# Attention and a gated feed-forward layer on one Trainium2 core: the planner's rules for VectorE and GpSimd rewritten

## The chip, the cores and the metric

The program runs on one NeuronCore of a Trainium2 chip. The core has TensorE (PE, matrix products), VectorE (DVE), ScalarE (ACT) and GpSimd (POOL) for elementwise work, and SyncE (SP), whose queue issues every transfer here. They work on SBUF and on PSUM, where TensorE leaves its results; GpSimd works on SBUF only. The metric is the device time of one execution in microseconds (us). The time before is 734.29 us, the median of 3 runs (733.88 to 735.38).

## The reference

```python
def _attn_ref(q, k, v):                       # 4 batches, 8 heads, 768 tokens, 64 wide
    block, window = (32, 16)
    k_sum = k.reshape(B, H, nb, block, D).max(axis=3)
    v_sum = v.reshape(B, H, nb, block, D).mean(axis=3)
    scores_l = scale * np.matmul(q, k.transpose(0, 1, 3, 2))      # used where |i - j| < window
    scores_s = scale * np.einsum('bhsd,bhnd->bhsn', q, k_sum) + np.log(block)
    ...
    a = softmax over [masked scores_l, scores_s]
    return np.matmul(a, np.concatenate([v, v_sum], axis=2))

def _moe_ref(x, w_gate, w_val, w_out):        # 3072 tokens, 512 -> 1536 -> 512; weights are float64
    g = x @ w_gate
    silu = g * (1.0 / (1.0 + np.exp(-g)))
    return (silu * (x @ w_val) @ w_out).astype(np.float32)
```

Each token attends to its neighbours within 16 places and to the 24 pooled blocks of its sequence. The result is the input `x` of a gated feed-forward layer.

## The kernel before

The four batches of the attention are four stages of the layer. Attention goes in 32 units: `k` counts half sequences (two per batch, 384 tokens), `u` counts pairs of heads. A unit is: the scores (`SC`, tile `sc`), per query tile a maximum with bias on VectorE (`ttr`, L467), exponentials on ScalarE (L481), the reciprocal of the sum (L499), a scaling of `p` by it (`nrm`, L502), transposes (`PP`, tile `pp`) that are copied out to `pt`, and the product with the values (`XO`, tile `xo`). Small copies put pooled keys (`kw<-ks`) and pooled values (`vw<-vs`) beside the windows.

The layer's operands are split into a high and a low part (`xh`/`xl`, `hh`/`hl`, the two halves of `w` and `o`), and a product is three matmuls. The float64 weights come as pairs of words, and five steps of `decode` turn each block into float32: one on ScalarE (L747) and four on VectorE (L751, L757, L764, L770), for twelve blocks `m_w` of 1024 columns and twelve `m_o` of 512. Then `split` makes `w` or `o`.

Batch 0 multiplies plainly (`u_plain`: `g` and `v` of 12 matmuls each, then `a` = silu(`g`) times `v`). Meanwhile `w_first` forms four sums and differences of the quarters of each `m_w` and stores them (`sf`, and `wa`). Batches 1 to 3 use these in a scheme that needs seven products instead of eight (`u_seven`, L888): the products `p` leave PSUM through VectorE steps that read PSUM (`v`, `u`, two of the `c`) and ScalarE copies (`s`), and the steps `c22` (`c<-v,u`), `a<-c,a`, `hh` and `hl` follow in SBUF. Before each of these batches `x_operands` builds the operands from the attention's result `xf` by differences and splits (`t`, `xf<-xf,xf`, `xh`, `xl`). Every third block `j`, `downs` multiplies by the output weights (L948, tile `acc`, six row tiles), and each result is added from PSUM into `part` (L335), which frees its PSUM bank.

The order is not the one in which the code stands. Each piece becomes a step of a plan, with the engines that can do it and a cost for each, and `order` calls `run` three times. `run` is a list scheduler: it gives every step an engine and a start by estimated costs, waits for buffers included, and instructions are then issued in the order of the starts. TensorE keeps two fixed lines (the layer's steps, and the attention's at its side) and takes whichever can start first. The other engines take, of the steps that are ready, the one with the earliest due time. A step that several engines can do goes to the one that would end it first, with a handicap per engine:

```python
BIAS = {DVE: 1.2, ACT: 0.6}
...
mine = soon + s.engines[e] + BIAS.get(e, 0)
if any(max(free[x], at[s]) + c + BIAS.get(x, 0) < mine - 1e-9 for x, c in s.engines.items() if x != e):
    continue
```

`cost` gives a step of two SBUF inputs and 384 columns 0.57 us on VectorE and 1.03 us on GpSimd. These numbers decide only the order and the engine; on the chip an engine works off its own queue in that order, waiting for the data that each instruction needs. Early in the program `warm_up` puts filler matmuls where the plan lets TensorE idle.

Of the kernel before, what the change touches and what calls it, by code (L numbers as in the profile page):

```python
# [197 lines left out]
def run(steps, line, late):  # L198
# [30 lines left out]
    while n:  # L229
        best = None  # L230
        for e, waiting in ready.items():
# [47 lines left out]
def body(ctx, tc, qP, kP, vT, vP, wgv, wo, bias, ident, mean, out):  # L279
# [68 lines left out]
    def add_dma(name, nbytes, out, in_, reads, writes):  # L348
        plan.add(name, {DMA: nbytes / 0.36e6}, lambda e: nc.sync.dma_start(out(), in_()), reads, writes)
# [30 lines left out]
    def a_pool_keys(b, u):  # L380
# [57 lines left out]
    def a_scores(k, u):  # L438
# [71 lines left out]
    def a_transposes(k, u):  # L510
# [6 lines left out]
        for g in range(2):  # L517
# [689 lines left out]
```

## Time and profile before

| | before |
|---|---|
| median of 3 runs | 734.29 us |
| profiled execution | 735.51 us, of which the span from first to last instruction is 733.7 us |
| TensorE busy | 691.4 us, 94% |
| VectorE busy | 457.6 us, 62% |
| ScalarE busy | 368.8 us, 50% |
| GpSimd busy | 408.0 us, 56% |
| DMA | 150.17 MB, mean 205 GB/s |
| chain that ended last | PE 58%, DVE 19%, DMA 9%, POOL 5%, ACT 5% |

Busy time is the union of an engine's instructions. Durations of neighbouring instructions on one engine overlap a little, so a step costs its engine the distance from start to start. In a group's row stand its count, its busy time, the mean of one instruction in nanoseconds, and the idle time of the engine before it with what ended it. The time of the instructions depends on the stage, so the tables of stretches matter more than the means over the run.

### The profile page before, as it was taken

What the parts mean: (1) busy time and instruction counts of PE and PEld (TensorE: products, weight loads), DVE (VectorE), ACT (ScalarE), POOL (GpSimd) and SP (SyncE); (2) the same over time, 40 slices, a digit from 0 to 9 for tenths busy, and PEclk for the clock granted to TensorE, in tenths of its full rate; (3) what the DMA queues carried; (4) which work ended last, traced back from release to release, by engine and by line L of the source; (5) the groups of instructions that cost most, each with busy time, mean ns of one, the idle gap of its engine ahead of it and who ended that gap; (6) DMA issues with size and microseconds to landing.
All of it is one profiled execution on the core that took longest, in us unless ns stands there. A gap on an engine that the chain in (4) does not pass through costs nothing.

```text
span 733.7 us, 13256 instructions
## 1 busy us (share of the span) xinstructions
PE 691.4 (94%) x4902; PEld 618.3 (84%) x4902; DVE 457.6 (62%) x995; ACT 368.8 (50%) x861; POOL 408.0 (56%) x387
## 2 busy tenths in 40 slices
PE   8787988999889999999999989999999999999997
PEld 7576876889779897897979879898989889989896
DVE  3799999888983858465755956343544942234342
ACT  3567744775655446565755527574754513322121
POOL 3767737656695946256564937263554834344342
PEclk9999899999999999999999999999999999999999
DMA  8999833758874359587583738284643546254422
GB/s 293 314 311 311 270 131 127 258 202 304 279 236 161 113 207 329 182 288 249 195 282 122 268 137 293 77 254 133 225 154 115 187 166 221 102 201 143 158 101 87
DMA packets 73329, 150.17 MB, mean 205 GB/s; under 512 B 25968, under 2 KB 48176, under 8 KB 67120
## 3 DMA queue, kind: packets, MB, share of 16 engines
q1 hardware_dynamic: 73264, 149.32, 59.8%
q8 instruction: 39, 0.64, 0.4%
q14 instruction: 26, 0.21, 0.1%
HBM read 114.70 MB, written 34.60 MB: 203 GB/s over the span
## 4 chain that ended last, share of the span: by engine, by line
PE 58%; DVE 19%; DMA 9%; POOL 5%; ACT 5%; issue 3%; SPq 1%; POOLq 0%; DVEq 0%; ACTq 0%
PE p L888 30%; PE acc L948 19%; DMA s<-sf 3%; PE g L865 2%; DVE m_o L764 2%; PE v L865 2%; PE xo L554 2%; PE sc L450 2%; DMA kt<-in_kP 2%; DVE xl_T L335 2%; PE pp L523 2%; DMA raw_o<-in_wo 1%; DVE m_w L764 1%; POOL m_w L335 1%; DVE m_w L751 1%
## 5 line engine op out<-in xcount | busy, mean ns | idle before, releaser
L948 PE MATMUL acc<-o,hh 128*128 128x512 f32 x576 | 186.5, 405 | 7.8 <-DVE part L335 6.1
L948 PEld LDWEIGHTS acc<-o,hh 128*128 128x128 f32 x576 | 106.4, 192 | 32.4 <-DVE part L335 7.4
L948 PE MATMUL acc<-o,hl 128*128 128x512 f32 x288 | 115.5, 401 | 6.0 <-POOL hl L335 5.9
L888 PE MATMUL p<-xh_T,s 128*128 128x384 f32 x432 | 120.1, 340 | 0.2 <-POOL s L335 0.2
L335 POOL TENSOR_TENSOR hl<-a,hh 128x384 fp32r<-128x384 f32 x88 | 99.7, 1140 | 30.0 <-ACT hh L330 16.1
L481 ACT ACTIVATE p<-p,nm 128x120 f32<-128x120 f32 x192 | 73.6, 385 | 31.1 <-DVE nm L467 30.6
L888 PE MATMUL p<-xh_B,wa 128*128 128x384 f32 x288 | 86.7, 341 | 0.0
L335 POOL TENSOR_TENSOR c<-v,u 128x384 f32<-128x384 f32 x31 | 32.7, 1056 | 91.1 <-DVE u L335 89.4
L335 POOL TENSOR_TENSOR a<-c,a 128x384 f32<-128x384 f32 x56 | 58.0, 1040 | 41.5 <-ACT a L847 23.5
L888 PEld LDWEIGHTS p<-xh_T,s 128*128 128x128 f32 x432 | 78.9, 188 | 1.6 <-issue 0.6
L335 DVE TENSOR_TENSOR part<-acc,part 128x512 f32<-128x512 f32 x72 | 48.1, 685 | 44.6 <-PE acc L948 44.5
L502 POOL TENSOR_TENSOR p<-p,ri 128x720 f32<-128x720 f32 x30 | 44.8, 1492 | 53.4 <-DVE ri L499 53.2
L335 DVE TENSOR_TENSOR c<-p,u 128x384 f32<-128x384 f32 x72 | 39.8, 554 | 54.1 <-PE p L888 52.9
L948 PEld LDWEIGHTS acc<-o,hl 128*128 128x128 f32 x288 | 55.2, 192 | 20.9 <-POOL hl L335 8.8
L888 PE MATMUL p<-xl_T,s 128*128 128x384 f32 x216 | 72.3, 335 | 0.0
L865 PE MATMUL g<-xh_B,w 128*128 128x384 f32 x192 | 56.4, 354 | 5.0 <-DVE w L335 2.2
L330 ACT COPY s<-p 128x384 f32<-128x384 f32 x60 | 28.5, 477 | 59.6 <-PE p L888 59.2
L467 DVE CUSTOM_DVE_ANT_0 p<-sc,bias_sb 128x120 f32<-128x120 f32 x192 | 41.6, 276 | 25.7 <-PE sc L450 25.3
L335 DVE TENSOR_TENSOR v<-p,s 128x384 f32<-128x384 f32 x36 | 20.0, 556 | 60.0 <-PE p L888 55.8
L335 POOL TENSOR_TENSOR m_w<-m_w 128x256 f32<-128x256 f32 x48 | 48.4, 1007 | 14.3 <-DVE w L335 11.1
L865 PE MATMUL v<-xh_B,w 128*128 128x384 f32 x192 | 55.0, 347 | 0.0
L888 PEld LDWEIGHTS p<-xh_B,wa 128*128 128x128 f32 x288 | 53.1, 188 | 1.6 <-issue 0.9
(118 smaller groups left out, 1514.1 us busy)
## 6 DMA issues: line engine op xcount, KB each, us to landing
wa<-wa SPq DMA_DIRECT2D x36, 768.0 KB, 4.3
s<-ss SPq DMA_DIRECT2D x24, 1024.0 KB, 7.6
raw_w<-in_wgv SPq DMA_DIRECT2D x12, 1024.0 KB, 6.9
ss<-s SPq DMA_DIRECT2D x12, 1024.0 KB, 5.8
wa<-w SPq DMA_DIRECT2D x12, 768.0 KB, 4.5
kw<-in_kP SPq DMA_DIRECT2D x28, 288.0 KB, 5.8
vw<-in_vP SPq DMA_DIRECT2D x28, 288.0 KB, 5.2
kt<-in_kP SPq DMA_DIRECT2D x16, 400.0 KB, 5.4
```

The costliest lines, as they stand in the source:

```text
L330: nc.scalar.copy(out, in_)
L335: vector[e].tensor_tensor(out=out, in0=a, in1=b, op=op)
L450: nc.tensor.matmul(make(sc[h])[s * QT : (s + 1) * QT, c * KC : (c + 1) * KC], make(q)[hs, qs], make(kw)[hs, i, :], start=True, stop=True,)
L467: nc.vector.tensor_tensor_reduce(out=make(p)[:, i, :], in0=make(sc[g])[:, c * KC : (c + 1) * KC], in1=make(bias_sb)[:, 0 if n == 0 else 2 ...
L481: nc.scalar.activation(out=make(p)[:, i, :], in_=make(p)[:, i, :], func=AF.Exp, scale=-1.0, bias=make(nm)[:, i : i + 1], accum_out=make(sm ...
L502: vector[e].tensor_tensor(out=make(p), in0=make(p), in1=make(ri).rearrange("p (n o) -> p n o", o=1).broadcast_to([P, NT, KC]), op=ALU.mult,)
L523: nc.tensor.transpose(make(pp)[:KC, c * P : (c + 1) * P], make(p)[:, g * NT // 2 + c, :], make(id_sb))
L554: nc.tensor.matmul(ps[hs, qs], v, make(pt)[:, h, qs], start=True, stop=True)
L764: lambda e: nc.vector.scalar_tensor_tensor(out=bits(), in0=high(), scalar=-0x40000000, in1=bits(), op0=ALU.bitwise_and, op1=ALU.bitwise_or ...
L865: nc.tensor.matmul(t[:, :TOK], a, x, start=u == 0 and n == 0, stop=u == NP - 1 and n == 2)
L888: nc.tensor.matmul(t[:, :TOK], a, x, start=first and kk == 0 and n == 0, stop=kk == 1 and n == 2, skip_group_check=not first,)
L948: nc.tensor.matmul(ps, a, w, start=j == js[0] and m == 0, stop=j == js[-1] and m == 2)
```

## The change

The planner gets a rule for VectorE and GpSimd. A step has a flag `port`: true if it reads nothing from PSUM (with exceptions set by hand: the pooling reductions and the reciprocal). In the plan, a GpSimd step starts only when the last VectorE step with `port` has ended (less 0.2 us), and such a VectorE step only when the last GpSimd step has. The choice of the engine looks at the start that this rule allows, and a step that would have to wait 1 us is ranked 1 us later. The handicaps become 0 for VectorE and ScalarE and 0.3 for GpSimd. The four weight sums become four steps, each for GpSimd or VectorE. Some costs are set anew (a transfer, TensorE's steps), filler matmuls are put in for the plan's first 110 us instead of 60, and the step `v` of `u_seven` is renamed.

```diff
-    def add(self, name, engines, do, reads=(), writes=(), table=None):
+    def add(self, name, engines, do, reads=(), writes=(), table=None, port=None):
         step = Step(name, engines, do, len(self.steps))
+        if port is None:
+            port = not any((b[0] if isinstance(b, tuple) else b).ring.pool == "psum" for b in reads)
+        step.port = port
         step.table, step.side, step.gate, step.slack = table, self.side, self.gate if self.side else None, self.slack if self.side else 0.0
 ...
 EARLY = 6.0
-BIAS = {DVE: 1.2, ACT: 0.6}
+BIAS = {DVE: 0.0, ACT: 0.0, POOL: 0.3}
+WAIT = 1.0
+HOLD = 0.2
 ...
     free = {PE: 0.0, DVE: 0.0, ACT: 0.0, POOL: 0.0, DMA: 0.0}
+    held = {DVE: 0.0, POOL: 0.0}
     table, place = None, [0, 0]
 ...
             else:
+                def start_of(x, s):
+                    t = max(free[x], at[s])
+                    if x == POOL:
+                        t = max(t, held[DVE])
+                    elif x == DVE and s.port:
+                        t = max(t, held[POOL])
+                    return t
+
                 soon = max(free[e], min(at[s] for s in waiting))
 ...
                         continue
+                    go = start_of(e, s)
                     if len(s.engines) > 1:
-                        mine = soon + s.engines[e] + BIAS.get(e, 0)
-                        if any(max(free[x], at[s]) + c + BIAS.get(x, 0) < mine - 1e-9 for x, c in s.engines.items() if x != e):
+                        mine = go + s.engines[e] + BIAS.get(e, 0)
+                        if any(start_of(x, s) + c + BIAS.get(x, 0) < mine - 1e-9 for x, c in s.engines.items() if x != e):
                             continue
-                    k = late[s] + (2.0 if s.table and s.table != table else 0.0)
+                    k = late[s] + (2.0 if s.table and s.table != table else 0.0) + WAIT * (go - soon)
                     if pick is None or (k, s.n) < (pick[1], pick[2].n):
-                        pick = (soon, k, s)
+                        pick = (go, k, s)
                 if pick is None:
 ...
         (start, _, s), e = best
+        if e == POOL or e == DVE and s.port:
+            start = max(start, held[POOL if e == DVE else DVE])
         for x in s.engines:
 ...
         s.idle = start - free[e]
+        if e == POOL or e == DVE and s.port:
+            held[e] = s.end - HOLD
         free[e] = s.end - (0.06 if e in (DVE, ACT, POOL) else 0.0)
 ...
     def add_dma(name, nbytes, out, in_, reads, writes):
-        plan.add(name, {DMA: nbytes / 0.36e6}, lambda e: nc.sync.dma_start(out(), in_()), reads, writes)
+        plan.add(name, {DMA: nbytes / 0.33e6}, lambda e: nc.sync.dma_start(out(), in_()), reads, writes)
 ...
-        def sums(e):
-            tt(e, at("A22"), at("A21"), at("A22"), ALU.add)
-            minus(e, at("A21"), at("A11"), at("A21"))
-            minus(e, at("A11"), at("A22"), at("A11"))
-            minus(e, at("A12"), at("A12"), at("A11"))
-
-        plan.add(f"sums w{j}", {POOL: 2.9}, sums, (), (m,))
+        for to, x, y, op in (("A22", "A21", "A22", ALU.add), ("A21", "A11", "A21", ALU.subtract), ("A11", "A22", "A11", ALU.subtract), ("A12", "A12", "A11", ALU.subtract)):
+            plan.add(
+                f"sum{to} w{j}", on((POOL, DVE), "tt", HALF), lambda e, to=to, x=x, y=y, op=op: tt(e, at(to), at(x), at(y), op), (), (m,)
+            )
         sf = SF[j] = buf("dram", f"sf{j}", [P, NC], f"sf{j}")
 ...
     for s in order(plan.steps):
-        if s.engine == PE and s.start < 60.0:
+        if s.engine == PE and s.start < 110.0:
             spare[0] = min(10, max(0, int((s.idle - 0.5) / 0.25)))
```

The costs of TensorE's steps change in the same manner as that of the transfer: `SC` 1.0 to 0.95, `PP` 0.36 to 0.38, `XO` 1.1 to 1.0, a product's matmul 0.1755 to 0.1745, one of `D` 0.231 to 0.229. `pool`, `vpool` and `rcp` get `port=False`.

In the built program VectorE has 1297 rows of instructions instead of 996, GpSimd 103 instead of 356, ScalarE 493 instead of 532, SP 281 in both. Three places show it.

VectorE in batch 0, where the first half of its rows of `u_plain` for the second 384 tokens stand (`m_o5` is the sixth block of output weights under `decode`, `a_0_0_1` the product of silu and `v` of block 0, second half). Before:

```order
L757 TENSOR_SCALAR m_o5_1122<-m_o5_1122 128x512
L764 SCALAR_TENSOR_TENSOR m_o5_1122<-raw_o5_706,m_o5_1122 128x512
L335 TENSOR_TENSOR xl_B22_0_1_1148<-xo_1_3_1125,xh_B22_0_1_1142 128x384
L770 SCALAR_TENSOR_TENSOR m_o5_1122<-raw_o5_706,m_o5_1122 128x512
L751 TENSOR_SCALAR m_o6_1151<-m_o6_1151 128x512
L757 TENSOR_SCALAR m_o6_1151<-m_o6_1151 128x512
L764 SCALAR_TENSOR_TENSOR m_o6_1151<-raw_o6_728,m_o6_1151 128x512
L770 SCALAR_TENSOR_TENSOR m_o6_1151<-raw_o6_728,m_o6_1151 128x512
L751 TENSOR_SCALAR m_o7_1188<-m_o7_1188 128x512
L757 TENSOR_SCALAR m_o7_1188<-m_o7_1188 128x512
L335 TENSOR_TENSOR a_0_0_1_1185<-v_0_1_1172,a_0_0_1_1185 128x384
L764 SCALAR_TENSOR_TENSOR m_o7_1188<-raw_o7_734,m_o7_1188 128x512
```

and now:

```order
L770 TENSOR_SCALAR m_o5_1173<-m_o5_1173 128x512
L354 TENSOR_TENSOR a_0_0_1_1170<-v_0_1_1157,a_0_0_1_1170 128x384
L776 TENSOR_SCALAR m_o5_1173<-m_o5_1173 128x512
L770 TENSOR_SCALAR m_o6_1177<-m_o6_1177 128x512
L783 SCALAR_TENSOR_TENSOR m_o5_1173<-raw_o5_775,m_o5_1173 128x512
L354 TENSOR_TENSOR hl_0_0_1_1216<-a_0_0_1_1170,hh_0_0_1_1197 128x384
L789 SCALAR_TENSOR_TENSOR m_o5_1173<-raw_o5_775,m_o5_1173 128x512
L776 TENSOR_SCALAR m_o6_1177<-m_o6_1177 128x512
L783 SCALAR_TENSOR_TENSOR m_o6_1177<-raw_o6_782,m_o6_1177 128x512
L354 TENSOR_TENSOR a_0_1_1_1219<-v_1_1_1203,a_0_1_1_1219 128x384
L354 TENSOR_TENSOR o5_1222<-m_o5_1173,o5_1222 128x512
L789 SCALAR_TENSOR_TENSOR m_o6_1177<-raw_o6_782,m_o6_1177 128x512
```

Against the product `a_0_0_1` the decode steps stand two blocks of output weights later, and the splits `hl` and `o5`, which were on GpSimd, stand between them.

VectorE before batch 2 (`xf_2_...`, `t3_2_...` and `xl_..._2_...` are that batch's operands, `a_1_11_1` and `hl_1_11_1` the last block of batch 1, `acc_1_3_0` its last product with the output weights). Before:

```order
L335 TENSOR_TENSOR xf_2_2_0_3746<-xf_2_2_0_3746,xf_2_0_0_3316 128x384
L335 TENSOR_TENSOR a_1_11_1_4717<-c22_1_11_4659,a_1_11_1_4717 128x384
L335 TENSOR_TENSOR xl_T4_2_0_4737<-xf_2_2_0_3746,xh_T4_2_0_4726 128x384
L335 TENSOR_TENSOR xl_B22_2_1_4743<-xf_2_3_1_4721,xh_B22_2_1_4728 128x384
L335 TENSOR_TENSOR xf_2_1_1_4332<-xf_2_1_1_4332,xf_2_1_0_3524 128x384
L335 TENSOR_TENSOR xf_2_1_0_3524<-xf_2_3_1_4721,xf_2_1_1_4332 128x384
L335 TENSOR_TENSOR xf_2_3_0_3928<-xf_2_3_0_3928,xf_2_1_0_3524 128x384
L335 TENSOR_TENSOR xl_T2_2_1_4775<-xf_2_1_0_3524,xh_T2_2_1_4767 128x384
L335 TENSOR_TENSOR part_1_0_3308<-acc_1_3_0_4710,part_1_0_3308 128x512
L335 TENSOR_TENSOR part_1_1_3311<-acc_1_3_1_4730,part_1_1_3311 128x512
L335 TENSOR_TENSOR part_1_2_3327<-acc_1_3_2_4747,part_1_2_3327 128x512
```

and now:

```order
L354 TENSOR_TENSOR t3_2_1_4736<-xf_2_3_1_4718,xf_2_1_1_4338 128x384
L354 TENSOR_TENSOR xl_T2_2_0_4740<-xf_2_0_0_3311,xh_T2_2_0_4705 128x384
L354 TENSOR_TENSOR hl_1_11_1_4751<-a_1_11_1_4720,hh_1_11_1_4738 128x384
L354 TENSOR_TENSOR xl_T3_2_1_4753<-t3_2_1_4736,xh_T3_2_1_4742 128x384
L354 TENSOR_TENSOR xf_2_1_1_4338<-xf_2_1_1_4338,xf_2_1_0_3531 128x384
L354 TENSOR_TENSOR xl_B21_2_1_4759<-xf_2_3_0_3936,xh_B21_2_1_4680 128x384
L354 TENSOR_TENSOR xf_2_1_0_3531<-xf_2_3_1_4718,xf_2_1_1_4338 128x384
L354 TENSOR_TENSOR part_1_0_3304<-acc_1_3_0_4709,part_1_0_3304 128x512
L354 TENSOR_TENSOR part_1_1_3316<-acc_1_3_1_4729,part_1_1_3316 128x512
L354 TENSOR_TENSOR part_1_2_3328<-acc_1_3_2_4744,part_1_2_3328 128x512
L354 TENSOR_TENSOR xl_T2_2_1_4790<-xf_2_1_0_3531,xh_T2_2_1_4775 128x384
L354 TENSOR_TENSOR xf_2_2_0_3741<-xf_2_2_0_3741,xf_2_0_0_3311 128x384
```

The three `part` stand ahead of the last operand steps, behind which they stood, and steps that GpSimd did (`t3`, `hl_1_11_1`, `xl_T3_2_1`) are among VectorE's.

GpSimd from the start of batch 1 (`c22`, `a` and `hl` of its first blocks; `s` a block's stored sums; `p_4_0` a unit's weights of attention). Before:

```order
L335 TENSOR_TENSOR c22_1_0_2969<-v_1_0_2959,u2_1_0_2967 128x384
L335 TENSOR_TENSOR a_1_0_0_2977<-c21_1_0_2985,a_1_0_0_2977 128x384
L335 TENSOR_TENSOR a_1_0_1_3006<-c22_1_0_2969,a_1_0_1_3006 128x384
L335 TENSOR_TENSOR hl_1_0_0_3037<-a_1_0_0_2977,hh_1_0_0_3020 128x384
L332 COPY kw_4_2_3043<-ks_2_2_2150 128x6x24
L335 TENSOR_TENSOR hl_1_0_1_3059<-a_1_0_1_3006,hh_1_0_1_3052 128x384
L335 TENSOR_TENSOR s_1_2_3022<-s_1_2_3022 128x1024
L502 TENSOR_TENSOR p_4_0_3015<-p_4_0_3015,ri_4_0_3118 128x720
L335 TENSOR_TENSOR a_1_1_0_3097<-c21_1_1_3099,a_1_1_0_3097 128x384
L335 TENSOR_TENSOR a_1_1_1_3123<-c22_1_1_3089,a_1_1_1_3123 128x384
L335 TENSOR_TENSOR hl_1_1_0_3172<-a_1_1_0_3097,hh_1_1_0_3168 128x384
L335 TENSOR_TENSOR hl_1_1_1_3185<-a_1_1_1_3123,hh_1_1_1_3174 128x384
```

and now:

```order
L354 TENSOR_TENSOR a_1_0_0_2973<-c21_1_0_2985,a_1_0_0_2973 128x384
L354 TENSOR_TENSOR hl_1_0_0_3024<-a_1_0_0_2973,hh_1_0_0_3015 128x384
L354 TENSOR_TENSOR a_1_0_1_3017<-c22_1_0_2965,a_1_0_1_3017 128x384
L354 TENSOR_TENSOR a_1_1_0_3103<-c21_1_1_3121,a_1_1_0_3103 128x384
L354 TENSOR_TENSOR a_1_1_1_3141<-c22_1_1_3094,a_1_1_1_3141 128x384
L351 COPY kw_5_0_3375<-ks_2_0_2893 128x6x24
L521 TENSOR_TENSOR p_4_2_3356<-p_4_2_3356,ri_4_2_3440 128x720
L351 COPY kw_5_1_3573<-ks_2_1_2931 128x6x24
L354 TENSOR_TENSOR s_1_5_3520<-s_1_5_3520 128x1024
L354 TENSOR_TENSOR c22_1_4_3615<-v_1_4_3563,u2_1_4_3605 128x384
L351 COPY vw_4_2_3318<-vs_2_3197 24x768
L354 TENSOR_TENSOR a_1_5_1_3761<-c22_1_5_3751,a_1_5_1_3761 128x384
```

What stood in the first list and is missing in the second is in VectorE's queue.

More of the change, by code (lines that the diff above doesn't have):

```diff
@@ L387, in do @@
             )
-        plan.add(f"pool({b},{u})", {DVE: 0.95}, do, (kt,), (ks,))
+        plan.add(f"pool({b},{u})", {DVE: 0.95}, do, (kt,), (ks,), port=False)
     def a_queries(k, u):
@@ L453, in do @@
                     )
-        plan.add(f"SC({k},{u})", {PE: 1.0}, do, (q, kw), sc)
+        plan.add(f"SC({k},{u})", {PE: 0.95}, do, (q, kw), sc)
     def a_softmax(k, u):
@@ L498, in a_softmax @@
         )
-        plan.add(f"rcp({k},{u})", {DVE: 0.18}, lambda e: nc.vector.reciprocal(out=make(ri), in_=make(sm)), (sm,), (ri,))
+        plan.add(f"rcp({k},{u})", {DVE: 0.18}, lambda e: nc.vector.reciprocal(out=make(ri), in_=make(sm)), (sm,), (ri,), port=False)
         def scale(e):
@@ L523, in turn @@
                     nc.tensor.transpose(make(pp)[:KC, c * P : (c + 1) * P], make(p)[:, g * NT // 2 + c, :], make(id_sb))
-            plan.add(f"PP{g}({k},{u})", {PE: 0.36}, turn, (p, id_sb), (pp,))
+            plan.add(f"PP{g}({k},{u})", {PE: 0.38}, turn, (p, id_sb), (pp,))
             add_copy(
@@ L554, in do @@
                     nc.tensor.matmul(ps[hs, qs], v, make(pt)[:, h, qs], start=True, stop=True)
-        plan.add(f"XO({k},{u})", {PE: 1.1}, do, reads, (xo,))
+        plan.add(f"XO({k},{u})", {PE: 1.0}, do, reads, (xo,))
     def load_first_values(x):
@@ L628, in do @@
             )
-        plan.add(f"vpool({b},{u})", {DVE: 0.95}, do, (vt,), (vr,))
+        plan.add(f"vpool({b},{u})", {DVE: 0.95}, do, (vt,), (vr,), port=False)
     def a_turn_values(b, u):
@@ L891, in do @@
                     )
-        plan.add(f"{name}({b},{j})", {PE: 6 * 0.1755}, do, [src] + sum(ops, []), (acc,))
+        plan.add(f"{name}({b},{j})", {PE: 6 * 0.1745}, do, [src] + sum(ops, []), (acc,))
     def u_seven(b, j):
@@ L907, in u_seven @@
         v = tmp("v")
-        add_tt(f"v({b},{j})", (DVE,), TOK, full(v), of(p5), full(s7), ALU.add, (p5, s7), (v,))
+        add_tt(f"vv({b},{j})", (DVE,), TOK, full(v), of(p5), full(s7), ALU.add, (p5, s7), (v,))
         product(b, j, "P6", "S2", "T2", p6, True, True)
@@ L952, in piece @@
             reads = sum(([*HH[b, j, hf], O[j]] for j in todo), [])
-            plan.add(f"D{n}({b},{g},{t})", {PE: 0.231 * 3 * len(todo)}, do, reads, (acc,))
+            plan.add(f"D{n}({b},{g},{t})", {PE: 0.229 * 3 * len(todo)}, do, reads, (acc,))
         def finish():
```

## The prediction

> **What bounds the kernel now.** I read the busy times of the page, then the table of busy time by stretch, then who releases TensorE, then single instructions where it idles.
>
> ```profile
> PE 691.4 (94%) x4902; PEld 618.3 (84%) x4902; DVE 457.6 (62%) x995; ACT 368.8 (50%) x861; POOL 408.0 (56%) x387
> ...
> 0.00:40.00 40.00, 31.70 (x401) 26.78 (x402) 22.74 (x80) 18.02 (x63) 19.95 (x38) 0.96 0.90 302
> 40.00:140.00 100.00, 84.62 (x603) 75.97 (x603) 96.46 (x171) 59.74 (x128) 67.76 (x55) 0.91 0.67 225
> 140.00:260.00 120.00, 113.92 (x870) 99.44 (x869) 91.73 (x198) 71.78 (x170) 81.68 (x71) 1.00 0.68 227
> 260.00:430.00 170.00, 163.68 (x1160) 144.24 (x1159) 111.55 (x248) 94.13 (x217) 97.18 (x85) 0.99 0.67 227
> 430.00:594.00 164.00, 161.44 (x1159) 144.71 (x1159) 85.22 (x220) 91.69 (x215) 87.76 (x86) 0.99 0.53 177
> 594.00:734.00 140.00, 136.04 (x717) 127.12 (x716) 49.88 (x83) 33.46 (x70) 53.72 (x52) 0.99 0.40 147
> ```
>
> The stretches (columns: start and end, length, busy time of PE, weight load, DVE, ACT, POOL, then granted clock, DMA share, GB/s) are my cuts: loading, the two parts of batch 0, then batches 1, 2, 3. TensorE is the bound nearly everywhere; the share of 62% for VectorE hides that it is full (96.46 of 100) from 40 to 140. There TensorE idles 100 − 84.62 = 15.4 and runs at clock 0.91, worth another 84.6 × 0.09 = 7.6: 23 us lost. Idle later: 6.1, 6.3, 2.6; the last batch has none but its tail. So what can be won is about 23 + 6 + 6 + 3 us plus the slow clock after long waits, in batch 0 mostly.
>
> Why VectorE is full is seen where GpSimd works beside it:
>
> ```profile
> 400.50 0.56 DVE L335 TENSOR_TENSOR c<-v,u 128x384 f32<-128x384 f32 x1
> ...
> 641.88 1.01 POOL L335 TENSOR_TENSOR a<-c,a 128x384 f32<-128x384 f32 x1 [1.13 <-DVE c L335]
> ...
> 417.06 1.33 POOL L335 TENSOR_TENSOR t<-xf,xf 128x384 f32<-128x384 f32 x1
> 418.35 1.33 POOL L335 TENSOR_TENSOR hl<-a,hh 128x384 fp32r<-128x384 f32 x1
> ...
> 414.88 1.35 DVE L335 TENSOR_TENSOR xf<-xf,xf 128x384 f32<-128x384 f32 x1 [0.45 <-POOL xl_B L335]
> 416.16 1.37 DVE L335 TENSOR_TENSOR a<-c,a 128x384 f32<-128x384 f32 x1
> 417.45 1.36 DVE L335 TENSOR_TENSOR xl_T<-xf,xh_T 128x384 fp32r<-128x384 f32 x1
> ...
> 423.77 1.87 DVE L335 TENSOR_TENSOR part<-acc,part 128x512 f32<-128x512 f32 x3
> ```
>
> The same 384-column step takes 0.56 on VectorE and 1.01 on GpSimd alone, 1.36 and 1.33 side by side, one pair every 1.29 us (start to start). Two such steps in a row on VectorE take 2 × 0.47 = 0.94 (0.56 less the overlap of about 0.09, seen at 96.95 to 97.42 below). So a pair is cheaper on VectorE alone, and VectorE loses 0.81 per step that meets one of GpSimd.
>
> By the Trainium skill (SBUF — State Buffer, "Who interferes with whom") the later of the two blocks until the other has finished. That would be 1.01 + 0.47 = 1.48 a pair; the trace has 1.29, so it agrees on the loss and not on its full size, and the 1.29 is used.
>
> **The change, part by part.** Counted in the two orders, GpSimd keeps 115 of 387 instructions. VectorE gets some 300 more: +81 `hl`, +47 `a<-c,a`, +29 `c<-v,u`, +28 scalings of `p`, +21 `pt`, +16 `vw`, +16 weight sums, and some 60 others.
>
> *First part of batch 0*, up to the ninth product of `a` with `v`: in the trace the last one before 140. The groups of these 140 us (busy, mean ns of one), and single steps:
>
> ```profile
> L764 DVE SCALAR_TENSOR_TENSOR m_o<-raw_o,m_o 128x512 int32<-128x512 int32 x12 | 16.9, 1405 | 0.2
> L770 DVE SCALAR_TENSOR_TENSOR m_o<-raw_o,m_o 128x512 int32<-128x512 int32 x12 | 10.0, 836 | 0.1
> L751 DVE TENSOR_SCALAR m_w<-m_w 128x1024 f32<-128x1024 f32 x7 | 9.0, 1290 | 1.7 <-ACT m_w L747 1.7
> L751 DVE TENSOR_SCALAR m_o<-m_o 128x512 f32<-128x512 f32 x12 | 8.2, 689 | 0.0
> L335 DVE TENSOR_TENSOR a<-v,a 128x384 f32<-128x384 f32 x9 | 4.9, 542 | 0.0
> ...
> 96.95 0.55 DVE L335 TENSOR_TENSOR xl_B<-xo,xh_B 128x384 fp32r<-128x384 f32 x1
> 97.42 0.68 DVE L770 SCALAR_TENSOR_TENSOR m_o<-raw_o,m_o 128x512 int32<-128x512 int32 x1
> 98.02 0.41 DVE L751 TENSOR_SCALAR m_o<-m_o 128x512 f32<-128x512 f32 x1
> ...
> 113.16 0.68 DVE L757 TENSOR_SCALAR m_w<-m_w 128x1024 int32<-128x1024 int32 x1
> ...
> 114.83 1.21 DVE L764 SCALAR_TENSOR_TENSOR m_w<-raw_w,m_w 128x1024 int32<-128x1024 int32 x1
> ```
>
> Relief: `m_o` 12 × (1.405 − 0.68) + 12 × (0.836 − 0.68) + 12 × (0.689 − 0.41) = 8.7 + 1.9 + 3.3; `m_w` 7 × (1.29 − 0.68) = 4.3. The other lines that meet GpSimd here, worked the same way, give some 10. Together 28 us of VectorE. Leaves the part: 16 of the 48 steps of `m_o`, 8 × 0.60 + 8 × 0.41 = 8. Enters: 6 scalings (720 columns, not seen alone: between the 0.60 of 512 and 1.13 of 1024 columns, both less the overlap, 0.8 taken), 4.8; `w` 3 × 1.13; `pt` 7 × 0.47; `o` 4 × 0.60; seven sums of 256 columns (not seen on VectorE; above zero and below 0.47, 0.33 taken), 2.3; `hl` 3 × 0.47; small ones 0.5; in all 18. Net −28 + 18 − 8 = −18 us. No wait of TensorE can give more than the 23. Two-engine separation exists only in the plan (the diff adds no wait between the two engines), so some meetings stay. I take 10; the ends are 0 and 20.
>
> *Second part of batch 0* (140 to 256):
>
> ```profile
> L764 DVE SCALAR_TENSOR_TENSOR m_w<-raw_w,m_w 128x1024 int32<-128x1024 int32 x6 | 8.7, 1446 | 0.1
> ...
> L757 DVE TENSOR_SCALAR m_w<-m_w 128x1024 int32<-128x1024 int32 x5 | 6.0, 1206 | 0.1
> L751 DVE TENSOR_SCALAR m_w<-m_w 128x1024 f32<-128x1024 f32 x5 | 5.8, 1161 | 0.2 <-ACT m_w L747 0.2
> L335 DVE TENSOR_TENSOR xl_B<-xf,xh_B 128x384 fp32r<-128x384 f32 x5 | 4.9, 1015 | 0.0
> ...
> L335 DVE TENSOR_TENSOR hl<-a,hh 128x384 fp32r<-128x384 f32 x2 | 3.6, 1785 | 0.8 <-ACT hh L330 0.8
> ```
>
> Relief 6 × 0.24 + 5 × (0.53 + 0.48) + 5 × 0.46 + 2 × 1.23 = 11, and some 5 in smaller groups: 16. Enters: `hl` 12, and `xf`, `t`, `xl_T` 11, and `pt` 5, at 0.47: 13; scalings 8 × 0.8; the 16 decode steps, 8; nine sums, 3; `vw` 5 × 0.5; `w`, `s`, `o`, 3; casts and copies, 1. Five pooling steps of 0.95 leave. Net 32 − 16: VectorE goes from 91.7 to about 108 of 120. Its slack shrinks from 28 to 12 us. TensorE idles 6.1 here now. I take 0; the ends are a gain of 5 and a loss of 8.
>
> *The two boundaries* (before batches 2 and 3, where the new input's operands are built):
>
> ```profile
> 424.50 0.80 PE L948 MATMUL acc<-o,hh 128*128 128x512 f32 x2 [2.74 <-DVE part L335]
> ...
> 424.50 5.31 PE acc L948 x15
> ...
> 500.78 3.45 PE acc L948 x15
> ...
> 588.17 0.73 PE L948 MATMUL acc<-o,hh 128*128 128x512 f32 x2 [2.56 <-DVE part L335]
> ```
>
> TensorE waits for an eviction (`part`) that stands at 423.77 behind eight SBUF steps begun at 414.88, 8.9 us. The wait is paid twice: the next fifteen matmuls take 5.31 instead of 3.45. That is 2.74 + 1.86 = 4.6 per boundary, 9.2 for both. In the new order the first three `part` stand ahead of five operand steps that they stood behind, and each step costs 0.47: nine steps and a copy, 4.7 us from 415, end near 420, before the wait begins (424.50 − 2.74 = 421.8). What is late next is the operand chain behind `part`. I take 7; ends 0 and 9.
>
> *Inside batches 1 and 2* (batch 1's groups and waits):
>
> ```profile
> L332 DVE CAST hh<-a 128x384 fp32r<-128x384 f32 x9 | 6.9, 773 | 6.5 <-POOL a L335 6.5
> ...
> L335 DVE TENSOR_TENSOR xf<-xf,xf 128x384 f32<-128x384 f32 x6 | 6.5, 1076 | 0.6 <-POOL xl_B L335 0.5
> ...
> PE acc L948 <- POOL hl L335: 2.5, 3, 1.2
> ```
>
> VectorE: 111.6 − 21 + 45 = 135 of 170, and 85.2 − 12 + 40 = 113 of 164. Of what enters, 40 and 50 steps cost 0.47, the rest as above; the relief is 9 × 0.4 + 6 × 0.53 = 7 from these two groups and 14 from nine smaller ones, and in batch 2 the same without the weights' share. TensorE's other idle time, 6.3 − 2.7 = 3.6 in batch 1, is mostly the wait for `hl`, now half as long. I take 1.5; ends −3 and 3.6. Batch 3: VectorE 50 + 24 of 140, nothing.
>
> *The sums in four steps* free the store `sf` and what SP holds behind it:
>
> ```profile
> SPq L349 <- POOL m_w L335: 34.1, 11, 6.2
> ```
>
> Behind that wait stand loads of `raw_o`, `kt` and `kw`. Their order changes only by places; it is paid by slack (DMA share 0.67). Longer fillers: 74 instead of 77 filler matmuls, in time that TensorE idles anyway.
>
> ```profile
> L983 PE MATMUL g<-warm 128*128 128x128 f32 x42 | 6.8, 326 | 0.0
> ```
>
> Each is two of these instructions, 6.8 / 21 = 0.32 us if that cover is gone. The changed TensorE costs and the renamed step act through the order alone. All at zero.
>
> Sum: 10 + 0 + 7 + 1.5 = 18.5, from the profiled execution's 735.5 (span 733.7 and 1.8 around it): 717. The median is 1.2 below the profiled one: 716.
>
> **The rivals.** *All of it arrives* (20 + 5 + 9 + 3.6 = 37): 698. For it: the 96.46. Against: VectorE at 90% in the second part.
>
> *Batch 0 only shifts its queue*: what the first part wins, the second loses to a full VectorE; the boundaries remain: 734 − 8 = 726. For it: 108 of 120, and 96 of 100 went with 23 lost.
>
> *Slower: the separation is not kept*, and VectorE has both its old losses and the new work. Place: 140 to 260. At half the relief there, 91.7 − 8 + 32 = 116 of 120, the fullness that cost 23 per 100 us; that is up to 15 lost beyond today's 6, while the first part gains 4 (−14 + 10) and the boundaries 3: 734 + 15 − 7 = 742. It decides once about half of GpSimd's steps still meet one. Against it: only 118 remain.
> The Trainium skill points this way (Perfetto Trace Analysis, "Optimizing Scalar/DVE Operations"): with VectorE saturated, work may be moved off it, even to GpSimd; this change does the reverse. It adds there that the shared read port may undo such a move, and the 1.36 against 0.56 bears the addition out.
>
> *No difference*: the loads (DMA share 0.90 to 40) and TensorE's fixed order set batch 0, and the boundary waits find another cause: 734.
>
> **How the numbers follow.** Forecast 0.47, all of it 0.13, only the boundaries 0.19, no difference 0.07, slower 0.14. Faster holds the first three, 0.79; 0.2% is about what a measurement here can tell. The range 703 to 735 leaves out the deepest of the second case and the slower one; the forecast's own range is 708 to 724 (first term 5 to 16, boundaries 4 to 9).
>
> **What would show it.** Right: GpSimd near 120 us busy, VectorE near 530; the `m_o` groups near 0.7 and 0.45; `hl` and `a` on VectorE near 0.56; no wait of 2 us for `part` before batches 2 and 3; TensorE's idle time between 40 and 140 halved. Wrong: SBUF steps of VectorE still near 1 us, or TensorE idling over 10 us between the ninth and the last product of batch 0, or new waits of TensorE for VectorE's evictions in batch 1.

## The result and the profile after

The changed kernel takes 697.3 us, the median of 4 runs (695.64 to 698.46); the kernel before, timed beside it, takes 734.84 (733.88 to 735.56). The ratio is 0.9488, with a 95% interval from 0.9464 to 0.9513: 37.5 us less, where 18.5 were forecast. The profiled execution took 695.64 us, with a span of 693.8.

The busy times of the page, and the stretches of the changed kernel (columns as before). The stretches are bounded by where the ninth product of `a` with `v` starts (before: 134.8, after: 115.0) and by where batches 1, 2 and 3 begin with their first `p`.

```profile
PE 676.6 (98%) x4918; PEld 612.9 (88%) x4918; DVE 543.0 (78%) x1296; ACT 350.2 (50%) x826; POOL 107.8 (16%) x115
...
0.00:40.00 40.00, 32.73 (x422) 28.77 (x423) 29.10 (x97) 21.34 (x69) 12.77 (x25) 1.00 0.96 318
40.00:115.00 75.00, 68.76 (x539) 63.36 (x539) 73.36 (x156) 47.20 (x103) 24.46 (x23) 0.98 0.80 270
115.00:235.00 120.00, 120.00 (x930) 106.60 (x930) 116.09 (x281) 78.32 (x182) 34.47 (x32) 1.00 0.66 221
235.00:394.00 159.00, 159.00 (x1156) 143.13 (x1156) 132.36 (x324) 86.60 (x205) 25.10 (x23) 1.00 0.77 258
394.00:553.00 159.00, 159.00 (x1157) 143.18 (x1156) 116.23 (x304) 84.65 (x202) 10.99 (x13) 1.00 0.54 182
```

The two parts of batch 0 of the kernel before at the same places of the program:

```profile
40.00:135.00 95.00, 80.28 (x562) 72.07 (x561) 92.06 (x156) 54.77 (x116) 63.62 (x51) 0.91 0.66 224
135.00:260.00 125.00, 118.26 (x911) 103.34 (x911) 96.12 (x213) 76.75 (x182) 85.82 (x76) 1.00 0.68 228
```

From 115 to 553 TensorE is busy without a gap at clock 1.00, though VectorE is at 116.09 of 120 in the second part of batch 0. All of TensorE's waits for another engine that are left lie in the first part; the longest are:

```profile
PE g L881 <- DVE w L354: 5.0, 1, 5.0
PE pp L542 <- DVE p L521: 2.1, 2, 1.5
PE pp L542 <- ACT p L500: 2.1, 1, 2.1
PE xo L573 <- ACT pt L349: 1.2, 2, 0.6
```

Lengths of the stages in the profiled executions, from these starts (the last column is the rest of the span):

| | first part | second part | batch 1 | batch 2 | batch 3 |
|---|---|---|---|---|---|
| before | 134.8 | 125.2 | 169.6 | 163.7 | 140.4 |
| after | 115.0 | 119.7 | 159.2 | 159.2 | 140.7 |
| gain | 19.8 | 5.6 | 10.4 | 4.5 | −0.3 |

The gains add up to 40.0, since these are the profiled executions; the medians differ by 37.5.

VectorE's steps got nearly as short as they are alone. The groups of the weights' decode over batch 0, after (busy, mean ns of one), and VectorE before batch 2 (start and duration):

```profile
L783 DVE SCALAR_TENSOR_TENSOR m_w<-raw_w,m_w 128x1024 int32<-128x1024 int32 x12 | 17.3, 1438 | 0.0
...
L783 DVE SCALAR_TENSOR_TENSOR m_o<-raw_o,m_o 128x512 int32<-128x512 int32 x12 | 9.2, 775 | 0.0
...
L770 DVE TENSOR_SCALAR m_w<-m_w 128x1024 f32<-128x1024 f32 x12 | 8.2, 684 | 1.3 <-ACT m_w L766 1.2
...
L770 DVE TENSOR_SCALAR m_o<-m_o 128x512 f32<-128x512 f32 x12 | 5.0, 426 | 0.0
...
381.95 1.37 DVE L354 TENSOR_TENSOR a<-c,a 128x384 f32<-128x384 f32 x1
...
388.39 1.87 DVE L354 TENSOR_TENSOR part<-acc,part 128x512 f32<-128x512 f32 x3
```

`m_o` fell from 1.405 and 0.689 to 0.775 and 0.426. Some meetings remain: 1.438 for `m_w` where 1.21 was seen alone, 1.37 for one `a`. The three `part` stand at 388.39 among operand steps, and no wait for them is left in TensorE's list.

### The profile page after: what moved, and what is told of

Read it like the earlier page. It is cut to its first block, busy times and chain, and to the rows that moved or that the text cites. A ratio compares the mean times of both kernels' runs of the same rounds, so it can differ in the third digit from the quotient of the medians.

```text
span 693.8 us, 13084 instructions
## 1 busy us (share of the span) xinstructions
PE 676.6 (98%) x4918; PEld 612.9 (88%) x4918; DVE 543.0 (78%) x1296; ACT 350.2 (50%) x826; POOL 107.8 (16%) x115
## 4 chain that ended last, share of the span: by engine, by line
PE 91%; DVE 5%; DMA 2%; ACT 1%; issue 1%; SPq 0%; ACTq 0%
PE p L904 39%; PE acc L964 28%; PE g L881 7%; PE v L881 7%; PE sc L469 3%; PE xo L573 3%; PE pp L542 2%; DMA q<-in_qP 2%; PE sc L999 1%; PE dummy L1006 1%; DVE w L354 1%; DVE pt L351 0%; ACT m_w L766 0%; DVE part L354 0%; DVE m_w L770 0%
## 5 line engine op out<-in xcount | busy, mean ns | idle before, releaser
L964 PE MATMUL acc<-o,hh 128*128 128x512 f32 x576 | 182.6, 398 | 0.0
L964 PEld LDWEIGHTS acc<-o,hh 128*128 128x128 f32 x576 | 104.7, 188 | 22.6 <-issue 1.4
L964 PE MATMUL acc<-o,hl 128*128 128x512 f32 x288 | 112.8, 392 | 0.0
L500 ACT ACTIVATE p<-p,nm 128x120 f32<-128x120 f32 x192 | 73.5, 385 | 20.6 <-DVE nm L486 20.2
L349 ACT COPY s<-p 128x384 f32<-128x384 f32 x52 | 24.9, 478 | 59.9 <-PE p L904 59.7
L349 ACT CAST hh<-a 128x384 fp32r<-128x384 f32 x53 | 27.1, 514 | 54.9 <-DVE a L354 53.8
L354 DVE TENSOR_TENSOR hl<-a,hh 128x384 fp32r<-128x384 f32 x89 | 51.2, 578 | 2.9 <-ACT hh L349 0.5
L904 PE MATMUL p<-xl_B,wa 128*128 128x384 f32 x144 | 48.3, 335 | 0.0
L904 PE MATMUL p<-xh_T,wa 128*128 128x384 f32 x144 | 42.7, 337 | 0.0
L904 PE MATMUL p<-xh_B,s 128*128 128x384 f32 x144 | 42.5, 335 | 0.0
```

Source lines behind the costliest of these rows:

```text
L349: nc.scalar.copy(out, in_)
L354: vector[e].tensor_tensor(out=out, in0=a, in1=b, op=op)
L500: nc.scalar.activation(out=make(p)[:, i, :], in_=make(p)[:, i, :], func=AF.Exp, scale=-1.0, bias=make(nm)[:, i : i + 1], accum_out=make(sm ...
L904: nc.tensor.matmul(t[:, :TOK], a, x, start=first and kk == 0 and n == 0, stop=kk == 1 and n == 2, skip_group_check=not first,)
L964: nc.tensor.matmul(ps, a, w, start=j == js[0] and m == 0, stop=j == js[-1] and m == 2)
```

## The experiments

Each kernel was timed against the kernel before in three rounds. Where the order differs from the changed kernel's and fillers go up to 110 us of the plan, none go ahead of the second piece of a product with the output weights, since they would break its sum. The stages in the tables are those of one profiled execution each.

### Which part of the change carries the gain

Theory A: the planner's choice of engine does it, by ending the meetings of VectorE's and GpSimd's SBUF steps. Rival D: the split sums, the cost numbers and the fillers carry a part. The old choice (e1) and no separation (e4) are the changed kernel with

```diff
                 def start_of(x, s):
                     t = max(free[x], at[s])
-                    if x == POOL:
-                        t = max(t, held[DVE])
-                    elif x == DVE and s.port:
-                        t = max(t, held[POOL])
                     return t
...
-        if e == POOL or e == DVE and s.port:
-            start = max(start, held[POOL if e == DVE else DVE])
```

and e1 also with

```diff
-BIAS = {DVE: 0.0, ACT: 0.0, POOL: 0.3}
+BIAS = {DVE: 1.2, ACT: 0.6}
```

The choice alone (e2) keeps all of the rule and the biases and takes sums, costs and fillers from before; the biases alone (e3) take the rule away too.

> The changed kernel with the old choice of engines (old biases of 1.2 and 0.6, no separation in the plan); sums in four steps, new cost numbers and longer fillers stay. GpSimd has 372 instructions in its order, before 356, changed 103. Theory A (the choice of engine is the cause, the meetings of the two engines' SBUF steps the mechanism): 734, within 4 us, TensorE idle 40 to 140 again near 15 us. Rival D (sums in steps, cost numbers and fillers carry a part, since they free stores and reorder loads): 715 to 722.

> The kernel before with the new choice of engines alone (biases and separation); sums in one step, old cost numbers, fillers to 60 us. GpSimd 96 instructions. Theory A: 697 within 4 us. Rival D: 712 to 718.

> The kernel before with the new biases alone, no separation in the plan. GpSimd 140 instructions. Theory A1 (the separation in the plan carries the gain; left to chance, about half of GpSimd's steps meet one of VectorE, 70 x 0.81 = 57 us of VectorE, most of it in batch 0, where VectorE is full): 715 to 722. Theory A2 (taking steps off GpSimd is what ends the meetings; the separation has only the last 40 steps to win, 20 x 0.81 = 16 us of VectorE, half of it in batch 0): 700 to 706.

> The changed kernel without the separation in the plan; new biases, sums in four steps, costs and fillers stay. GpSimd 144 instructions. A1: 712 to 720. A2: 698 to 705. If it is at or below 697, the separation wins nothing and the mechanism is only how much GpSimd is given.

| | median us | ratio to before, 95% | first | second | batch 1 | batch 2 |
|---|---|---|---|---|---|---|
| after | 697.3 | 0.9464 to 0.9513 | 115.0 | 119.7 | 159.2 | 159.2 |
| e1 old choice | 727.69 | 0.9876 to 0.9933 | 133.6 | 124.0 | 168.3 | 161.8 |
| e2 choice alone | 707.1 | 0.9575 to 0.9669 | 124.0 | 121.6 | 159.3 | 159.2 |
| e3 biases alone | 709.11 | 0.9614 to 0.9698 | 123.1 | 122.5 | 160.8 | 159.2 |
| e4 no separation | 708.25 | 0.9614 to 0.9669 | 120.9 | 126.2 | 161.0 | 159.7 |

Neither theory holds alone. The choice brings 28 of the 37.5, and nearly all of batches 1 and 2. Two thirds come from the biases alone, with no separation at all (26). The other edits bring 7 without the choice (e1) and 10 with it (e2 to after). The separation wins 11 beside the other edits (e4 to after, intervals apart), and 2 without them (e3 to e2, intervals overlapping): it needs something among them. Both e3 and e4 lie between the figures of A1 and A2: fewer steps on GpSimd end most of the loss, and the separation adds to it. Without the separation VectorE is busy 548.6 us instead of 543.0 with 36 instructions fewer (e4), so slower steps of VectorE are a part of the 11 us; how large a part was not separated.

### What the separation needs

```diff
-            plan.add(f"sum{to} w{j}", on((POOL, DVE), "tt", HALF), ...)
+        plan.add(f"sums w{j}", {POOL: 2.9}, sums, (), (m,))
```

is e5. In e12 the four steps stay, on `(POOL,)` alone; in e14 it is one step, with `{POOL: 2.9, DVE: 1.73}`. e6 has `s.start < 60.0` for the fillers, e7 the old cost numbers.

> The changed kernel with the weight sums as one GpSimd step again. Theory A (the first part of batch 0 is bound by VectorE's busy time, and the sums are 16 x 0.33 = 5 us on VectorE and 32 x about 1 us of blocks on GpSimd that the plan can place between VectorE's steps; as one step of 2.9 they keep VectorE or are met by it longer): 699 to 703. Rival O (only a new order by another number; the ten us that the edits beside the choice of engine bring are not the sums): 697 within 2 us.

> The changed kernel with fillers up to 60 us of the plan instead of 110. Theory A (fillers hold the clock of TensorE between 60 and 90 us; the clock from 40 to the ninth product is 0.98 after, and was 0.91 to 0.96 in the three kernels with the new choice and 60 or 110): 698 to 702, clock 0.94 to 0.96 there. Rival O (TensorE has no idle time behind 80 us that fillers could fill): 697 within 1.5 us.

> The changed kernel with the old cost numbers of the loads and of TensorE's steps. Theory C (the loads at 0.33 instead of 0.36 GB per ms make the plan start loads earlier or keep VectorE off steps whose data are late; VectorE idled 17 of the first 40 us before and 11 after): 702 to 707, the loss before the ninth product. Rival O: 697 within 2 us.

> The changed kernel with the sums in four steps, all of them on GpSimd (no choice of engine). One step of four instructions made it 12 us longer. Theory P (short steps are what lets the plan put them between VectorE's): 697 to 701. Theory E (the choice of VectorE for a third of them, 16 of 48, is what helps): 704 to 710.

> The changed kernel with the sums as one step of four instructions that may go to GpSimd or to VectorE. One step on GpSimd alone: 709; four steps on GpSimd alone: 699. Theory P (the length of the step is what hurts: the plan cannot place 2.9 us beside VectorE's steps): what goes to GpSimd is as hard to place, but some can go to VectorE: 700 to 704. If it is 706 or more, the four separate steps are the cause whatever the engine; if 697 to 699, the free choice is as good as the split.

| | median us | ratio to before, 95% | first | second |
|---|---|---|---|---|
| e5 one step, GpSimd | 709.07 | 0.9626 to 0.9701 | 131.1 | 119.7 |
| e12 four steps, GpSimd | 698.69 | 0.9489 to 0.9547 | 118.3 | 121.7 |
| e14 one step, either | 699.79 | 0.9462 to 0.9557 | 116.2 | 122.6 |
| e6 fillers to 60 us | 697.71 | 0.9467 to 0.9527 | 114.4 | 119.7 |
| e7 old costs | 701.90 | 0.9533 to 0.9599 | 118.2 | 121.4 |

The sums are the partner. One step for GpSimd alone costs 12 us; four short ones, or one that may go to VectorE, give it back, so short steps (theory P) are enough, and the free choice of engine alone is nearly as good (699.79, between the two figures named for e14). e2, another order with the separation and the sums in one step, is 10 us longer. Where the 12 go is seen in what VectorE waited for from 40 to 121 in e5, whose profiled execution, 712.5, was the slowest of its four (total, times, longest):

```profile
DVE ks L404 <- DMA kt<-in_kP: 5.4, 1, 5.4
DVE p L486 <- PE sc L469: 4.2, 1, 4.2
DVE w L354 <- ACT w L349: 3.2, 1, 3.2
DVE m_w L770 <- ACT m_w L766: 2.2, 1, 2.2
```

Together 15.0; the changed kernel has 1.5 in all from 40 to 115. Then TensorE waits too:

```profile
PE acc L968 <- ACT o L349: 7.8, 1, 7.8
```

Followed back, this wait begins with VectorE's wait for the load `kt` (start, duration, idle time before and what ended it):

```profile
88.22 0.95 DVE L404 TENSOR_REDUCE ks<-kt 128x24 f32<-128x768 f32 x1 [5.41 <-DMA kt<-in_kP]
89.43 0.66 DVE L354 TENSOR_TENSOR hl<-a,hh 128x384 fp32r<-128x384 f32 x1
90.12 0.49 ACT L866 ACTIVATE a<-g 128x384 f32<-128x384 f32 x1 [6.14 <-DVE hl L354]
92.58 0.62 ACT L349 CAST o<-m_o 128x512 fp32r<-128x512 f32 x1
93.26 0.80 PE L968 MATMUL acc<-o,hh 128*128 128x512 f32 x1 [7.77 <-ACT o L349]
```

VectorE stands in its queue for the load, and `hl` stands behind it; ScalarE waits for `hl`, and TensorE for the `o` that ScalarE makes next. SP issued the load at 79.71, just after the previous `ks` of VectorE had ended (78.75 to 79.69); the store of the sums ahead of the load on SP was issued by 78.86. So it is rather the place of VectorE's own steps than the store that held the load. That the long step does this by its place in the order is argued from these rows; the other three waits were not followed. Theory A's mechanism for e5 (more busy time) is not what happened: up to 131, where the ninth product starts, VectorE was busy 103.4 us against 102.5 in the changed kernel, and stood idle 15 us longer. From 40 us to there:

```profile
40.00:131.00 91.00, 77.80 (x574) 71.00 (x575) 76.94 (x168) 52.80 (x117) 28.50 (x27) 0.91 0.73 234
```

The fillers do nothing. For the old costs the question is what any new order costs.

### What a new order alone does

e15 sets `SLACK = 1.5` and loads at `0.34e6`; e16 sets `HOLD = 0.4`.

> The changed kernel with two of the plan's own numbers set otherwise (the slack of the side steps 1.5 instead of 2.5; loads at 0.34 instead of 0.33): the order is drawn anew by the same rules. What the time does here is what a new draw alone does: 693 to 700 if orders by the same rules are alike, so that the 4.6 of the old cost numbers and the 12 of the sums are more than a draw; 690 or 705 if a draw alone is worth so much.

> The changed kernel with the plan's allowance for an overlap of two steps at 0.4 instead of 0.2 us: another draw by the same rules, GpSimd 122 instructions. 694 to 701 by the same reasoning; above 703 if the planned distance between the two engines' steps is itself what counts.

Measured 698.47 (ratio 0.9429 to 0.9544) and 701.19 (0.948 to 0.9583). In these two draws a new order by the same rules moves the time by 1 to 4 us, so the 4.6 of e7 and the 1.4 of e12 are not told from a draw; the 12 of e5 and the 11 of e4 lie clear of both. No kernel tried is better than the changed one.

### Does a full VectorE cost TensorE time?

The prediction took nothing for the second part because VectorE would be nearly full there. Dummy additions were put into the changed kernel's own order, on a tile of their own:

```diff
+        if s.name in extra:
+            for _ in range(6):
+                tt(DVE, make(idle), make(idle), make(idle), ALU.add)
```

`extra` are the products `a` of blocks 4 to 11 in batch 0. e8 has six, e9 three on VectorE, e10 three on GpSimd, and e11 six on GpSimd behind 16 products of batch 3.

> The changed kernel in its own order, with six additions of 256 columns on a tile of their own on VectorE behind each of the 16 products a of weights 4 to 11 in batch 0: 96 x about 0.34 = 33 us more of VectorE where it is busy 116 of 120 us. The outputs are the same. Theory F (of the prediction: a full VectorE costs TensorE what exceeds the stretch): the second part is 33 - 4 = 29 us longer, 726. Theory S (VectorE there works ahead, on decodes and operands that are not yet wanted, so that part of the 33 us is taken from its lead): under 15 us longer, below 712.

> As the kernel with six additions of 256 columns on VectorE behind each of 16 products of batch 0, but three: 48 x about 0.34 = 16 us more of VectorE there. Six, 33 us, made it 41 us longer. Theory F (VectorE sets the pace of the second part, and TensorE only just keeps up): 12 to 20 us longer, 709 to 717. Theory S (there is some lead, and only what exceeds it is paid): the first 10 us or more are free, under 8 us longer, below 705.

> The changed kernel in its own order with three additions of 256 columns on a tile of their own on GpSimd behind each of the same 16 products: 48 x 0.73 = 35 us more of GpSimd, which is busy 34 of 120 us there. The outputs are the same. Theory M (a GpSimd step takes VectorE's time where it meets SBUF steps of VectorE: at most its own length less what VectorE would have waited, by the rows of before 0.81 for 1.01): VectorE 20 to 28 us more busy, by the run of 33 us on VectorE 15 to 30 us longer, 712 to 727. Rival N (two engines may overlap at little cost; the choice of engine wins by something else): within 4 us of 697.

> The same on GpSimd, but 96 additions that start when GpSimd's own last step is done (about 547 us) and last some 70 to 100 us, mostly in batch 3, where VectorE is busy 76 of 141. Theory M with slack: VectorE's SBUF steps there take up to twice as long and VectorE is 20 to 40 us more busy, but TensorE waits under 3 us: 697 to 701. If TensorE waits more, single late steps matter and not the stretch's total: above 703.

| | median us | VectorE busy more | GpSimd busy more | second part longer |
|---|---|---|---|---|
| e9, VectorE x48 | 715.05 | 20.1 | | 17.5 |
| e8, VectorE x96 | 738.56 | 40.9 | | 40.8 |
| e10, GpSimd x48 | 707.22 | 12.3 | 41.4 | 7.9 |
| e11, GpSimd x96 in batch 3 | 698.32 | 8.6 | 66.7 | 0.0 |

(The ratios to before are 0.9712 to 0.9761, 1.0032 to 1.0079, 0.96 to 0.9656 and 0.9484 to 0.9533. On VectorE an addition added 0.43 us of busy time and not 0.34, so the doses were 20 and 41 us and not 16 and 33; all go through one tile, so that each needs the one before it, which may be why.) The second parts of e9 and e8, up to batch 1:

```profile
115.00:254.00 139.00, 127.38 (x951) 111.36 (x944) 137.13 (x329) 78.60 (x182) 29.66 (x33) 0.96 0.57 187
...
117.00:278.00 161.00, 132.20 (x932) 114.32 (x931) 157.12 (x378) 78.47 (x182) 28.24 (x32) 0.93 0.50 165
```

VectorE is 98 to 99% busy in both, and every further us is paid, about one for one: theory F. At 116.09 of 120 nothing was paid. The changed kernel sits at the point where TensorE and VectorE are both full in that part, and behind it there is no lead to spend. That a fuller VectorE costs nothing up to this point is shown for this order alone: the next experiment has an order in which TensorE waits beside a VectorE that is 90% busy.

On GpSimd, 41 us cost VectorE 12.3, less than the 20 to 28 expected, and the time 9.9, above N's 4 and below M's 15: the mechanism of M at a smaller price, 0.30 us of VectorE for one of GpSimd (0.13 in e11). In batch 3, where VectorE has slack, the same kind of load costs the stage nothing (140.4 against 140.7).

### Without GpSimd

```diff
-BIAS = {DVE: 0.0, ACT: 0.0, POOL: 0.3}
+BIAS = {DVE: 0.0, ACT: 0.0, POOL: 5.0}
```

> The changed kernel with a bias of 5.0 for GpSimd instead of 0.3: its order holds 7 instructions, VectorE's 1383 (1297). No step of the two engines can meet. Theory B (balance: VectorE sets the pace of batch 0, each us more costs one; GpSimd's 72 us of batch 0 are worth some 35 to 40 us on VectorE, less 0.3 us of VectorE for each of the 72, 22 us): 10 to 20 us longer, 707 to 717, all of it in batch 0. Theory Z (meetings are the whole cost, and none is best): 697 or less.

Measured 712.31 (0.9635 to 0.9729), 15 us longer, first part 120.6, second 131.9. The size is theory B's, and Z falls: no meeting at all is worse than few. The reading is only half B's (118 to 250 us, nearly the second part):

```profile
118.00:250.00 132.00, 124.40 (x963) 110.81 (x962) 118.59 (x307) 88.10 (x197) 0.00 (x0) 0.97 0.64 207
```

VectorE has 13 us idle there, and of the 7.6 that TensorE idles one wait for a scaled `p` is the most:

```profile
PE pp L542 <- DVE p L521: 4.6, 1, 4.6
```

So the loss is partly the place of single steps in VectorE's queue; how much was not separated.

## Why the prediction was wrong

The direction, the places and, in the main, the mechanism were right; the sum was half of what came. The case that came is the rival *All of it arrives*, 698, which got a chance of 0.13 and lies outside the range of 703 to 735. Its terms of 20, 5, 9 and 3.6 were met nearly one by one (19.8, 5.6, about 9 and 5.8). Term by term:

- **First part of batch 0: "I take 10; the ends are 0 and 20".** This is the step that failed most: it measured 19.8. Runs with the same order up to there (e8, e9, e11) have 116.8 to 117.7 for the 115.0, so the term is 17 to 20. The discount, from 18 to 10, stood for meetings that would remain. For `m_o` few did (0.775 and 0.426, alone 0.68 and 0.41). But the discount was too deep even for a kernel that leaves the separation out: e4 has 120.9, a gain of 13.9 against the 10 taken. Something else came in that had no term. VectorE's busy time up to the ninth product fell from 22.74 + 92.06 = 114.8 to 29.10 + 73.36 = 102.5, by 12.3, less than the net of 18. But its idle time fell too, from 20.2 to 12.5: the moved steps went into gaps of the loading stretch, where VectorE was busy 22.74 of 40 and I looked only for meetings. 12.3 + 7.7 = 20. That the gaps took the moved steps is read from these totals; no run tests it alone. By the runs, the choice of engine gives about 11 of the 20 (e2, e3), the short sums and the other edits 2 to 3 more without the separation (e4), and the rest came only with both.
- **Second part: "I take 0", because VectorE's slack shrinks.** It measured 5.6, just over the upper end. VectorE went higher than I had said (116 of 120, not 108), and TensorE still lost nothing. The wrong step is the price of fullness: I took the 23 us lost beside a full VectorE in the first part as what fullness costs. The doses show that in this order a VectorE at 116 of 120 costs nothing, and each us beyond costs one. In the second part of before, VectorE had 29 us to spare and TensorE idled 6.7, for single steps that were late: 4.8 of VectorE, 1.3 of GpSimd and 0.6 of ScalarE. Without the separation the part gains nothing (e4: 126.2, and before 125.2); there the term of 0 would have fitted. The two longest of the waits of before, which are gone after the change:

```profile
PE xo L554 <- DVE vw L332: 2.1, 1, 2.1
PE acc L948 <- POOL hl L335: 1.3, 1, 1.3
```

- **Boundaries: took 7, ends 0 and 9.** The stage of batch 2 gained 4.5, and the priced wait before batch 3 with the slow matmuls behind it was 4.6: TensorE's idle 2.6 went to 0, and its busy time fell by the rest. The wait before batch 2 is gone as well and lies in batch 1's gain. So the priced 9.2 fits, and lowering it to 7 was needless.
- **Inside batches 1 and 2: took 1.5, upper end 3.6.** Batch 1 gained 10.4 − 4.6 = 5.8, batch 2 nothing. The size was off: I charged the second payment of a wait (slow matmuls) at the boundaries only. In batch 1 TensorE's idle 6.3 went to 0, and its busy time fell by 10.4 − 6.3 = 4.1, of which the boundary's 1.86 is a part.
- **Sums at zero: wrong in this company.** Undone, they cost 12 us (e5). I had looked at the transfers behind SP's wait, and not at what one GpSimd step of 2.9 us does to a plan that keeps VectorE's steps away from it. Fillers at zero: right (e6). Costs at zero: not told from a new draw.
- ***Slower: the separation is not kept*.** A `hl` on VectorE takes 578 ns on average, so the separation held in the main. But the rival's 742 would not have come without it either: e4 leaves the separation out, `hl` takes 634, and the time is 708. The 15 us in that sum do not follow from its own rate: 23 per 100 us over 120 us, less today's 6, are 22.

The signs named in advance came out: GpSimd 107.8 us (near 120), VectorE 543.0 (near 530), no 2 us wait for `part`, no new waits in batch 1. TensorE's idle time from 40 us to the ninth product was more than halved, from 14.7 to 6.2.

All four terms were set too low. Only the first was argued from meetings that would remain; and the kernels without the separation (e3, e4), where they do remain, still gained 26 to 27 us, more than the 18.5. So the forecast was short in what taking steps off GpSimd brings by itself, and not only in how well the separation holds.

## What to carry to other kernels

Ask of a nearly full engine whether its work still fits the time in which its partner is full. In the changed kernel's order a high share cost nothing below that point, and each us beyond it cost one, so measure the point with dummy steps before discounting a gain; in another order single late steps cost time earlier (without GpSimd, at 118 of 132). Moving steps from GpSimd back to VectorE can pay even where VectorE looks saturated, since part of its busy time is the meeting itself; but leave GpSimd what fits between. When a planner gets a rule that keeps two engines apart, look at its long steps first, and compare against a second order drawn by the same rules before crediting an edit with 4 us.

## What the hardware showed that was not expected

Which VectorE steps a GpSimd stream slows is very selective. The groups on VectorE while e11's additions run on GpSimd (547 to 626), and then the same groups of the changed kernel (546 to 625):

```profile
L354 DVE TENSOR_TENSOR hl<-a,hh 128x384 fp32r<-128x384 f32 x13 | 11.7, 898 | 0.9
L354 DVE TENSOR_TENSOR a<-c,a 128x384 f32<-128x384 f32 x12 | 9.3, 774 | 0.6
L354 DVE TENSOR_TENSOR part<-acc,part 128x512 f32<-128x512 f32 x12 | 8.1, 687 | 5.3 <-PE acc L964 5.3
L354 DVE TENSOR_TENSOR c<-p,u 128x384 f32<-128x384 f32 x12 | 6.6, 553 | 3.0 <-PE p L904 3.0
...
L351 DVE CAST hh<-a 128x384 fp32r<-128x384 f32 x6 | 3.9, 653 | 0.2
```

```profile
L354 DVE TENSOR_TENSOR part<-acc,part 128x512 f32<-128x512 f32 x12 | 8.1, 687 | 6.7 <-PE acc L964 6.7
L354 DVE TENSOR_TENSOR a<-c,a 128x384 f32<-128x384 f32 x12 | 6.7, 559 | 0.6
L354 DVE TENSOR_TENSOR hl<-a,hh 128x384 fp32r<-128x384 f32 x12 | 6.7, 559 | 0.9
L354 DVE TENSOR_TENSOR c<-p,u 128x384 f32<-128x384 f32 x12 | 6.6, 554 | 5.6 <-PE p L904 5.6
...
L351 DVE CAST hh<-a 128x384 fp32r<-128x384 f32 x6 | 2.2, 359 | 0.2
```

Steps with both inputs in SBUF go from 559 to 898 and 774 ns, and the cast `hh`, with its one input in SBUF, from 359 to 653; those that read one input from PSUM stay within a nanosecond (687, 553). The plan's flag `port`, which asks whether a step reads PSUM, draws the line where these rows do. It is part of why 41 us of GpSimd cost only 12.3 in e10's second part; but only about 38 of VectorE's 116 us there are in steps that read PSUM, so the low price is not explained by them alone. The Trainium skill (SBUF — State Buffer, "Who interferes with whom") says that a VectorE instruction with two SBUF inputs contends with a GpSimd instruction that reads SBUF, and that one with at most one SBUF input does not, outside the modes in which VectorE uses two ports. The rows of `hl`, `a`, `part` and `c` agree; `hh` agrees only if the cast ran in such a mode, which no row shows.
